# A seven-unit Strassen step for two chunks of the second sequence matrix, with its operand sums made by DMAs

## The chip, the cores and the metric

The kernel runs on one NeuronCore of a Trainium2 chip. The metric is the device time of one execution in microseconds, taken as the median of several runs. The engines are named as in the profile: PE (TensorE, matmuls), PEld (its weight loads), DVE (VectorE), ACT (ScalarE), POOL (GpSimd) and SP (SyncE, which here only issues DMAs). Each engine works off its own instructions in the order in which the program lists them, and waits on semaphores for the others.

## The reference

The function mixes two branches for S = 2048 tokens of width D = 640:

```python
x = A_x
g = sigmoid((x * gate_w).sum(-1, keepdims=True))
a = FNet(x)          # Real(DFT_seq(DFT_hid(x)))
b = PEER(x)          # product-key expert retrieval
return g * a + (1 - g) * b
```

FNet is `y = Cr (x Dr^T) - Ci (x Di^T)` with the sequence matrices Cr, Ci (2048 x 2048) and the hidden matrices Dr, Di (640 x 640). PEER makes 32 queries per token from `w_q` (640 x 32 x 256), scores each half against 16 keys, takes the best two of each half and the best two of their sums, and adds up the 2 x 32 chosen experts: `softmax(score) * gelu(x . u[e]) * v[e]`, with 256 experts of width 640.

## The kernel before

All products are done in fp32r in three parts. An operand is split by `split` (L121) into a high part (ACT rounds a copy, L123) and a low part (POOL or DVE subtracts, L124), and `mm3` (L126) multiplies high by high, high by low and low by high: three matmuls of 512 columns, L128 to L130, called a product here.

**The sequence products.** The kernel multiplies the sequence matrices with x first: for each matrix w (0 real, 1 imaginary) and each chunk c of 512 output columns, 16 pieces s. Each is one product for each of the five d tiles of x, into five PSUM banks (`seq_piece`, L201). That makes 128 pieces in `pieces` (L152). x stands split in SBUF (`X`). A piece is loaded by SP into one of five buffers `wf` (`load_piece`, L155, five pieces ahead) and split by ACT and POOL three pieces ahead (`split_piece`, L163) into a ring `WS` of four places. When a chunk ends, ACT copies the five banks to the staging tile `ST` (L218). DVE multiplies them by the gate row `grow` (`gate_piece`, L187), and ACT issues the stores to the DRAM tensor `pd[w, c]` one piece later (`store_piece`, L196).

**What lies between the pieces.** The program is one list written out by hand: `at(n, f)` puts f behind piece n. Up to piece 30 the queries' weights are folded with the keys. From N0 = 31 the score stage runs, 40 pieces long, five for each pair p of 128-token tiles. Behind each of the last four of the five stands one half of a score (`score_half`, five products, evacuated by ACT at L429), and behind the last `u_pair`, the product with the experts' `u`, and the split of the next tiles of x transposed (`split_xT`, ACT and POOL). DVE picks the best two (`topk`, L443 to L454). From N1 = 71 the hidden matrices are loaded and split into `DD` (`split_dd`, POOL). When the rows of the choices are in place (`rows`, DMA transposes issued by SP), the generator `experts` (L564) starts. DVE builds one-hot tiles (`build`, L572, three operations of 1024 columns, L579 to L581), PE multiplies them with 32-column matmuls (`use`, L599, line L607, one or two builds in a group), and ACT takes the sums out of the bank (L588).

**The pump.** What is not placed by `at` comes from `Pump`. Each product calls `run_bg(0.68)`, which adds 0.68 times `share` (0.95, or 1.25 while the experts run) to a credit. While the credit is positive the next step of the generators is put into the program, and its cost (3.3 for a build) is taken off. Other work of DVE takes its own cost off with `bg.credit -= ...`.

**The hidden products** come last, from L939 on. For each half b of the columns there is a Strassen step of seven units (`UNITS`, L671), with operand sums made by DVE (`add_a`, L747) and splits five steps ahead into a ring of six. The last pieces prepare it: `make_sums` and `split_sums` from 14 pieces before the end.

Of the kernel before, what the change touches and what calls it, by code (L numbers as in the profile page):

```python
# [16 lines left out]
P = 128  # L17
# [8 lines left out]
NP = NT // 2  # L26
TC = 512
NC = S // TC
NPC = 2 * NC * NT
KD = D // P  # L30
HALF = D // 2
NG = HH // 8
# [4 lines left out]
KX = KD + 1  # L37
NSTEP = 7 * KX
AHEAD = 5


class Pump:
# [49 lines left out]
def gated_mix_kernel(ctx: ExitStack, tc: tile.TileContext, xT, xn, dreT, dimT, wsre, wsim, wq, kT, uT, vv, gw, out):  # L92
# [25 lines left out]
    def stage():  # L118
        return ST[:, rotate("st", 5)]

    def split(f, h, l, eng):  # L121

        nc.scalar.activation(h, f, AF.Copy)  # L123
        eng.tensor_sub(l, f, h.bitcast(F32))  # L124
# [6 lines left out]

    pd = {(w, c): dram.tile([KD, P, TC], F32, name=f"pd{w}{c}", tag=f"pd{w}{c}") for w in range(2) for c in range(NC)}
    actd = dram.tile([2, P, S], F32, name="actd")
    gd = dram.tile([2, 2, 2, 2, E, E, P], F32, name="gd")
    gdr = dram.tile([S], F32, name="gdr")
    bg = Pump()
# [12 lines left out]

    pieces = [(w, c, s) for w in range(2) for c in range(NC) for s in range(NT)]  # L152
    pf, psp, X, xr = {}, {}, {}, {}

    def load_piece(n):  # L155
        if n < NPC:
            w, c, s = pieces[n]
            pf[n] = big.tile([P, TC], F32, name="wf", tag="wf", bufs=5)
            nc.sync.dma_start(pf[n], (wsre, wsim)[w][c, s])

    WS = big.tile([P, 4, 2, TC], F32R, name="WS", tag="WS")

    def split_piece(n, eng=nc.gpsimd):  # L163
        if n < NPC:
            psp[n] = WS[:, n % 4, 0], WS[:, n % 4, 1]
            split(pf.pop(n), *psp[n], eng)


    then = {}
# [31 lines left out]
    def seq_piece(n):  # L201
        w, c, s = pieces[n]
        if s == 0:
            banks[:] = [bank(d) for d in range(KD)]
# [8 lines left out]
        for d in range(KD):  # L213
            ds = slice(d * P, (d + 1) * P)
            mm3(banks[d], X[s][:, 0, ds], X[s][:, 1, ds], h, l, s == 0, s == NT - 1)
            if s == NT - 1:
                staged[n // NT, d] = f = stage()
                nc.scalar.activation(f, banks[d], AF.Copy)  # L218
            run_bg(0.68)

    for q in range(2 * NC):
        n = NT * (q + 1)
# [15 lines left out]
    def split_x(s):  # L238

        if s < NT:  # L240
            X[s] = big.tile([P, 2, D], F32R, name="X", tag=f"X{s}")
            f = xr[s // 2][:, s % 2]
            if s:
                split(f, X[s][:, 0], X[s][:, 1], nc.vector)
                return
            psp[0] = h, l = WS[:, 0, 0], WS[:, 0, 1]
            c = slice(0, 2 * P)
            split(f[:, c], X[0][:, 0, c], X[0][:, 1, c], nc.vector)
            split(pf.pop(0), h, l, nc.vector)
            c = slice(2 * P, D)  # L250
            split(f[:, c], X[0][:, 0, c], X[0][:, 1, c], nc.vector)

# [7 lines left out]
    pf[0] = big.tile([P, TC], F32, name="wf", tag="wf", bufs=5)  # L260
    nc.scalar.dma_start(pf[0], wsre[0, 0])
# [275 lines left out]
    def u_pair(p):  # L537
# [9 lines left out]
        for n in range(2):  # L547
            nc.scalar.dma_start(actd[n][:, 2 * p * P:2 * (p + 1) * P], act[:, n])

    for p in range(NP):  # L550
# [13 lines left out]
    def experts():  # L564
# [33 lines left out]

        def use(group):  # L599
            shape = (P, 16, E * 2)  # L600
            t = bank(7, shape) if last_part else ps_s(shape)
            for a, (g, c, s) in enumerate(group):
                pt, qt = (HOT[s // 2][:, s % 2, n].rearrange("p (m c j) -> p m c j", m=16, j=2) for n in range(2))
                for m in range(16):
                    for j in range(2):
                        r = slice(64 * (m % 2) + 32 * j, 64 * (m % 2) + 32 * j + 32)
                        nc.tensor.matmul(t[r, 8 * a + m // 2, :], pt[:, m, :, j], qt[:, m, :, j], start=True,  # L607
                                         stop=True)
# [121 lines left out]
    def take(key):  # L730
        if raw_tags:
            t, n = raw_tags.pop(0)
            if t == "wf":
                raw_free.append(big.tile([P, TC], F32, name="ra", tag=t, bufs=5))
# [101 lines left out]
    def step(m):  # L836
        b, (u, k) = m // NSTEP, divmod(m % NSTEP, KX)
        what = UNITS[u]
        if k == 0:
            if what in ("a11", "s1"):  # L840
                roles["W"] = bank(0)
            if what in ("a12", "a22"):
                roles["Z"] = [bank(1), bank(2)]
            if what == "s1":
                roles["Y"] = [bank(3), bank(4)]
            if what == "a11":
                roles["X"] = [bank(5), bank(6)]
# [142 lines left out]
```

## Time and profile before

| | us |
|---|---|
| median of 3 runs | 773.79 |
| lowest, highest | 772.95, 775.86 |
| the profiled execution | 773.85 |
| its span, first to last instruction | 772.1 |
| PE busy | 766.7 |
| DVE busy | 516.2 |
| POOL busy | 346.5 |
| ACT busy | 287.3 |

The time is that of one launch; the span is what lies between the first and the last instruction of the profile, 1.75 us less. A row of the groups gives line, engine and operation, the tiles written and read, count, then busy time and mean ns of one, then the engine's idle time just before and what ended it. A row of the timeline gives start, duration, engine, line, operation and tiles; `x4` means that four stand together, and the bracket tells how long the engine had idled and for whom. `SPq` and `ACTq` are DMAs issued by SP and ACT. A row of the stages gives start and end, length, busy time (and instructions) of PE, PEld, DVE, ACT and POOL, granted clock, DMA share and GB/s.

### The profile page before, as it was taken

How to read it: one execution, taken by the hardware profiler on the slowest of the kernel's cores; microseconds unless marked ns; L12 is line 12 of the kernel's file. 1: busy time of each engine (PE TensorE's matmuls, PEld its weight loads, DVE VectorE, ACT ScalarE, POOL GpSimd, SP SyncE). 2: the span in 40 equal slices, each digit the busy share in tenths (PEclk: the TensorE clock that was granted, in tenths of full speed). 3: DMA queues.
4: the chain of work that ended last, by engine and by line, in shares of the span. 5: the costliest groups of instructions: out<-in, count | busy, mean ns of one | idle time of the engine just before them, and what ended most of it. 6: DMA issues, size and time to landing. Idle time of an engine off the chain costs nothing.

```text
span 772.1 us, 11964 instructions
## 1 busy us (share of the span) xinstructions
PE 766.7 (99%) x4616; PEld 620.3 (80%) x4616; DVE 516.2 (67%) x611; ACT 287.3 (37%) x470; POOL 346.5 (45%) x235
## 2 busy tenths in 40 slices
PE   9999999999999999999999999999999999999997
PEld 6777677888888888888888888777788888788886
DVE  7642122276888698579988592677677789747761
ACT  5334324322214432353343462332243453543341
POOL 4522224315143242325242875343446765577253
PEclk9999999999999999999999999999999999999999
DMA  9976985603030440223325454453565586686411
GB/s 343 375 259 191 315 317 191 213 0 117 14 102 25 149 147 15 84 67 130 120 54 169 138 157 122 97 153 89 143 187 169 184 296 218 204 252 220 128 54 70
DMA packets 86953, 121.21 MB, mean 157 GB/s; under 512 B 33136, under 2 KB 40432, under 8 KB 86896
## 3 DMA queue, kind: packets, MB, share of 16 engines
q1 hardware_dynamic: 57360, 100.64, 39.7%
q10 hardware_dynamic: 29536, 19.81, 8.1%
q8 instruction: 36, 0.59, 0.3%
q14 instruction: 21, 0.17, 0.1%
HBM read 98.91 MB, written 19.93 MB: 154 GB/s over the span
## 4 chain that ended last, share of the span: by engine, by line
PE 98%; ACT 1%; POOL 0%; issue 0%; DVE 0%; ACTq 0%; DVEq 0%
PE b L128 31%; PE b L129 31%; PE b L130 31%; PE b L326 2%; PE b L607 1%; PE b L338 1%; PE b L211 1%; PE b L278 0%; POOL WS L124 0%; ACT L396 0%; ACT WS L123 0%; ACT ST L806 0%; ACT wp L332 0%; ACT WP L123 0%; ACT ST L218 0%
## 5 line engine op out<-in xcount | busy, mean ns | idle before, releaser
L124 POOL TENSOR_TENSOR WS<-wf,WS 128x512 fp32r<-128x512 f32 x126 | 189.6, 1509 | 279.3 <-ACT WS L123 250.3
L128 PE MATMUL b<-WS,X 128*128 128x512 f32 x635 | 251.2, 396 | 0.2 <-ACT ST L218 0.2
L129 PE MATMUL b<-WS,X 128*128 128x512 f32 x635 | 247.6, 390 | 0.0
L130 PE MATMUL b<-WS,X 128*128 128x512 f32 x635 | 247.5, 390 | 0.0
L128 PEld LDWEIGHTS b<-WS,X 128*128 128x128 f32 x635 | 119.2, 188 | 33.4 <-issue 7.3
L130 PEld LDWEIGHTS b<-WS,X 128*128 128x128 f32 x635 | 119.2, 188 | 25.4
L129 PEld LDWEIGHTS b<-WS,X 128*128 128x128 f32 x635 | 119.3, 188 | 23.5
L123 ACT ACTIVATE WS<-wf 128x512 fp32r<-128x512 f32 x128 | 80.6, 630 | 113.7 <-PE b L130 57.2
L443 DVE TENSOR_REDUCE mm<-sc 128x64 f32<-128x1024 f32 x32 | 39.0, 1219 | 46.3 <-ACT sc L429 45.7
L124 POOL TENSOR_TENSOR xl<-xf,xh 128x640 fp32r<-128x640 f32 x16 | 33.6, 2123 | 70.4 <-ACT xh L123 64.0
L124 POOL TENSOR_TENSOR WS<-ra,WS 128x512 fp32r<-128x512 f32 x40 | 59.7, 1512 | 12.0 <-ACT WS L123 12.0
L130 PE MATMUL b<-WU,xl 128*128 128x512 f32 x160 | 62.2, 389 | 0.0
L128 PE MATMUL b<-WU,xh 128*128 128x512 f32 x160 | 62.2, 389 | 0.0
L129 PE MATMUL b<-WU,xh 128*128 128x512 f32 x160 | 62.2, 389 | 0.0
L429 ACT ACTIVATE sc<-b 128x512 f32<-128x512 f32 x32 | 21.1, 661 | 100.4 <-PE b L130 93.5
L579 DVE TENSOR_TENSOR hot<-rows,wtab 128x1024 f16<-128x1024 f16 x32 | 30.0, 938 | 36.9 <-PE b L607 36.9
L123 ACT ACTIVATE WS<-ra 128x512 fp32r<-128x512 f32 x56 | 34.8, 630 | 51.8 <-PE b L130 29.8
L124 POOL TENSOR_TENSOR WP<-ra,WP 128x512 fp32r<-128x512 f32 x20 | 32.5, 1636 | 45.2 <-ACT WP L123 45.1
L749 DVE TENSOR_TENSOR ra<-ra 128x512 f32<-128x512 f32 x48 | 45.6, 1002 | 4.2 <-POOL WP L124 4.2
L192 DVE SCALAR_TENSOR_TENSOR ST<-ST,grow 128x512 f32<-128x512 f32 x40 | 37.1, 992 | 15.9 <-DMA grow<-gdr 15.9
L341 DVE TENSOR_TENSOR WU<-b,WU 128x512 fp32r<-128x512 f32 (+1 forms) x16 | 7.8, 490 | 57.2 <-ACT WU L340 57.2
L445 DVE TENSOR_TENSOR eq<-sc,mm 128x1024 f16<-128x1024 f32 x32 | 44.4, 1388 | 1.1
(132 smaller groups left out, 1182.4 us busy)
## 6 DMA issues: line engine op xcount, KB each, us to landing
wq<-in_wq SPq DMA_DIRECT2D x32, 640.0 KB, 6.7
ra<-pd SPq DMA_DIRECT2D x70, 256.0 KB, 3.7
wf<-in_wsim SPq DMA_DIRECT2D x64, 256.0 KB, 2.9
wf<-in_wsre SPq DMA_DIRECT2D x63, 256.0 KB, 5.4
pd<-ST ACTq DMA_DIRECT2D x40, 256.0 KB, 3.1
xf<-in_xT SPq DMA_DIRECT2D x16, 320.0 KB, 3.2
xr<-in_xn SPq DMA_DIRECT2D x15, 320.0 KB, 6.4
out_y<-ST ACTq DMA_DIRECT2D x7, 512.0 KB, 3.8
```

The source lines that it names most:

```text
L123: nc.scalar.activation(h, f, AF.Copy)
L124: eng.tensor_sub(l, f, h.bitcast(F32))
L128: nc.tensor.matmul(o, wh, ah, start=first, stop=False, skip_group_check=more)
L129: nc.tensor.matmul(o, wh, al, start=False, stop=False, skip_group_check=more)
L130: nc.tensor.matmul(o, wl, ah, start=False, stop=last, skip_group_check=more)
L192: nc.vector.scalar_tensor_tensor(f, f, -1.0 if w else 1.0, g, op0=OP.mult, op1=OP.mult)
L326: nc.tensor.matmul(ps[32 * j:32 * j + 32, :HALF], kp[:, 8 * G // H, r, :], w[:, j], start=(r == 0), stop=(r == 1))
L429: nc.scalar.activation(scs[i].rearrange("p h e -> p (h e)")[:, c], ps, AF.Copy)
L443: nc.vector.tensor_reduce(m, sc, op=OP.max, axis=AX.X)
L445: nc.vector.tensor_tensor(eq, sc, m[:, :, None].to_broadcast([P, HH, E]), op=OP.is_equal)
L579: nc.vector.tensor_tensor(pt, row(0), wt, op=OP.is_equal)
L749: nc.vector.tensor_add(take((b, o, k)) if f is not None else raw[b, o, k], raw[b, o, k] if f is None else f, raw[b, what, k])
```

## The change

The chunks are taken in another order: the four of the first matrix, then chunk 2 of the second, then chunks 0 and 1 of the second together, then chunk 3. The pair of chunks is a 2 x 2 block problem: output chunk (0, 1) times the half of the s tiles (0 to 7, 8 to 15). d tiles 0 and 1 against 2 and 3 of x make the other operand's halves. It is done with seven products of half blocks instead of eight, the units `QUNITS`, each with eight steps k of two d tiles. d tile 4 is done as before, a third product in the steps of four units. So 32 pieces become 56 steps (`quad_step`), and the list has 152 entries instead of 128 (Q0 = 80 to Q1 = 136 are the steps).

The units need sums of blocks of the sequence matrix (four, `sd`) and of x (four, `td`). They are made in the score stage, one k for each pair of tiles (`sums_part`). Two `wf` buffers are loaded by SP, ACT negates one, POOL issues DMAs that add a block from DRAM onto a buffer (`accum_op`), and SP stores each finished sum to DRAM. The sums of x are four subtractions on DVE, stored by one DMA. In the steps the sums are loaded like pieces, those of x in a ring of five, and split by ACT with POOL or DVE.

Beside that: the `wf` buffers become a queue of tags, to which two are added when the experts start, and the steps and later pieces are loaded seven ahead. The experts' sums always use bank 7. The last part of `DD` is split by DVE. The last chunk uses banks 3, 4, 5, 6, 0, and the hidden products swap two pairs of banks.

```diff
+HN = NT // 2
+Q0 = 5 * NT
+Q1 = Q0 + 7 * HN
+NPC = Q1 + NT
+QUNITS = ("a11", "a12", "s1", "s2", "s4", "s3", "a22")
...
+    order = ((0, 0), (0, 1), (0, 2), (0, 3), (1, 2))
+    pieces = [(w, c, s) for w, c in order for s in range(NT)] + [None] * (Q1 - Q0) + [(1, 3, s) for s in range(NT)]
...
     def load_piece(n):
-        if n < NPC:
-            w, c, s = pieces[n]
-            pf[n] = big.tile([P, TC], F32, name="wf", tag="wf", bufs=5)
-            nc.sync.dma_start(pf[n], (wsre, wsim)[w][c, s])
+        nonlocal loaded
+        while loaded <= min(n, NPC - 1):
+            pf[loaded] = wf_tile("wf")
+            nc.sync.dma_start(pf[loaded][0], source(loaded))
+            load_t(loaded)
+            loaded += 1
...
     def split_piece(n, eng=nc.gpsimd):
         if n < NPC:
             psp[n] = WS[:, n % 4, 0], WS[:, n % 4, 1]
-            split(pf.pop(n), *psp[n], eng)
+            f, tag = pf.pop(n)
+            if Q0 <= n < Q1 and unit(n)[0] in ("s1", "s2", "s4") and n % 3 == 0:
+                eng = nc.vector
+                bg.credit -= 0.9
+            split(f, *psp[n], eng)
+            wf_tags.append(tag)
+            split_t(n)
...
-        load_piece(n + 5)
+        load_piece(n + (7 if p3 else 5))
...
+    def split_t(n):
+        if t_index(n) is None:
+            return
+        m = qs["m"] % 4
+        qs["m"] += 1
+        f = tq[n]
+        tq[n] = [qs["hl"][m // 2][:, m % 2, a] for a in range(2)]
+        split(f, *tq[n], nc.vector)
+        bg.credit -= 0.5
...
+    def q_out(name, o, r, dp):
+        f, g = qres[name], grow[NC + r]
+        for a in range(2):
+            nc.vector.tensor_tensor(f[:, a], f[:, a], qrole[o][a], op=OP.add)
+            nc.vector.scalar_tensor_tensor(f[:, a], f[:, a], -1.0, g, op0=OP.mult, op1=OP.mult)
+        bg.credit -= 2.8
+        nc.scalar.dma_start(pd[1, r][2 * dp:2 * dp + 2].rearrange("d p t -> p d t"), f)
...
+    def quad_step(n):
+        what, k = unit(n)
...
+        load_piece(n + 7)
+        split_piece(n + 3)
+        h, l = psp.pop(n)
+        o = {"a11": "X", "a12": "Z", "s1": "Y", "s2": "X", "s4": "Y", "s3": "X", "a22": "Z"}[what]
...
+        for d in ds:
+            if d < 2:
+                c = slice(d * P, (d + 1) * P)
+                mm3(qrole[o][d], t[0][:, c], t[1][:, c], h, l, k == 0 and not more, end, more)
+            else:
+                c = slice(4 * P, KD * P)
+                mm3(qrole["W"], wx[:, 0, c], wx[:, 1, c], h, l, k == 0 and low, end and what != "s3", what == "a12")
+            run_bg(0.68)
+        if end:
+            q_post(what)
...
+    def sums_add(f, r, s):
+        nc.gpsimd.dma_start(f, wsim[r, s], accum_op=OP.add)
...
+    def sums_part(k, i):
+        if i == 0:
+            sums_load(k)
+        elif i == 1:
+            sums_neg(k)
+            sums_add(sb[k], 1, k + HN)
+            sums_x(k)
+        elif i == 2:
+            sums_add(sa[k], 1, k)
+            sums_store(sb[k], 0, k)
+            nc.sync.dma_start(td[k].rearrange("p j c -> p (j c)"), sx.pop(k).rearrange("p n c -> p (n c)"))
+        elif i == 3:
+            sums_store(sa[k], 2, k)
+        elif i == 4:
+            sums_add(sa[k], 1, k + HN)
+        elif i == 5:
+            sums_store(sa[k], 1, k)
+        elif i == 6:
+            sums_neg(k)
+        elif i == 7:
+            sums_add(sa[k], 0, k + HN)
+        elif i == 8:
+            sums_store(sa[k], 3, k)
...
     for p in range(NP):
         n = N0 + 5 * p
-        for a in range(4):
-            at(n + 1 + a, score_half, 2 * p + a // 2, a % 2)
+        for a in range(5):
+            at(n + a, sums_part, p, 2 * a)
+            if a:
+                at(n + a, score_half, 2 * p + (a - 1) // 2, (a - 1) % 2)
+            at(n + a, sums_part, p, 2 * a + 1)
...
-            t = bank(7, shape) if last_part else ps_s(shape)
+            t = bank(7, shape)
...
-        split(draw[m][:, a], DD[:, w, 0, k], DD[:, w, 1, k], nc.gpsimd)
+        split(draw[m][:, a], DD[:, w, 0, k], DD[:, w, 1, k], nc.vector if m == KD - 1 else nc.gpsimd)
```

`q_post` stands at a unit's end. It copies banks to `ST` with ACT (units a11, s1, s2, s3) or calls `q_out` (a12, s4, s3, a22); after a12 and a22, d tile 4 goes out as well.

More of the change, by code (lines that the diff above doesn't have):

```diff
@@ L148, in gated_mix_kernel, with wf_tile, unit, source @@
     gt = const.tile([P, NT], F32)
-    pieces = [(w, c, s) for w in range(2) for c in range(NC) for s in range(NT)]
+    order = ((0, 0), (0, 1), (0, 2), (0, 3), (1, 2))
+    pieces = [(w, c, s) for w, c in order for s in range(NT)] + [None] * (Q1 - Q0) + [(1, 3, s) for s in range(NT)]
     pf, psp, X, xr = {}, {}, {}, {}
-    def load_piece(n):
-        if n < NPC:
-            w, c, s = pieces[n]
-            pf[n] = big.tile([P, TC], F32, name="wf", tag="wf", bufs=5)
-            nc.sync.dma_start(pf[n], (wsre, wsim)[w][c, s])
+    wf_tags = deque((big, f"wf{n}") for n in range(5))
+    def wf_tile(name):
+        pool, tag = wf_tags.popleft()
+        return pool.tile([P, TC], F32, name=name, tag=tag), (pool, tag)
+    def unit(n):
+        u, k = divmod(n - Q0, HN)
+        return QUNITS[u], k
+    def source(n):
+        if not Q0 <= n < Q1:
+            w, c, s = pieces[n]
+            return (wsre, wsim)[w][c, s]
+        what, k = unit(n)
+        if what[0] == "s":
+            return sd[int(what[1]) - 1, k]
+        return wsim[int(what[1]) - 1, k + HN * (int(what[2]) - 1)]
+    loaded = 0
+    def load_piece(n):
+        nonlocal loaded
[4 more added lines that the diff above has]
+            loaded += 1
     WS = big.tile([P, 4, 2, TC], F32R, name="WS", tag="WS")
@@ L203, in seq_piece @@
         if s == 0:
[L204 to L205 removed]
+            banks[:] = [bank(d) for d in ((3, 4, 5, 6, 0) if n >= Q1 else range(KD))]
+        load_piece(n + (7 if p3 else 5))
         split_piece(n + 3)
@@ L212, in seq_piece @@
             return
-        for d in range(KD):
+        for d in ((4, 0, 1, 2, 3) if n == NPC - 1 else range(KD)):
             ds = slice(d * P, (d + 1) * P)
@@ L216, in seq_piece, with t_index, load_t @@
             if s == NT - 1:
-                staged[n // NT, d] = f = stage()
+                staged[w * NC + c, d] = f = stage()
                 nc.scalar.activation(f, banks[d], AF.Copy)
             run_bg(0.68)
-    for q in range(2 * NC):
-        n = NT * (q + 1)
+    tq, qs = {}, {}
+    def t_index(n):
+        what = unit(n)[0] if Q0 <= n < Q1 else None
+        return {"s1": 0, "s3": 1, "a22": 2, "s2": 3}.get(what)
+    def load_t(n):
+        j = t_index(n)
+        if j is None:
+            return
+        if not qs:
+            qs["raw"] = big.tile([P, 5, 2 * P], F32, name="tr", tag="xl")
+            qs["hl"] = [big.tile([P, 2, 2, 2 * P], F32R, name="tq", tag=t) for t in ("xf", "xh")]
+            qs["n"] = qs["m"] = 0
+        tq[n] = qs["raw"][:, qs["n"] % 5]
+        qs["n"] += 1
+        nc.sync.dma_start(tq[n], td[unit(n)[1], :, j])
@@ new lines, in q_post @@
+    def q_post(what):
+        if what == "a11":
+            nc.scalar.activation(qres["w"], qrole["W"], AF.Copy)
+            q_copy("c", "X")
+        elif what == "a12":
+            f = p3.tile([P, TC], F32, name="wrow")
+            nc.vector.scalar_tensor_tensor(f, qrole["W"], -1.0, grow[NC], op0=OP.mult, op1=OP.mult)
+            nc.scalar.dma_start(pd[1, 0][4], f)
+            q_out("c", "Z", 0, 0)
+        elif what == "s1":
+            q_copy("c22", "Y")
+        elif what == "s2":
+            q_copy("c", "X")
+        elif what == "s4":
+            q_out("c", "Y", 0, 1)
+            grow.pop(NC)
+        elif what == "s3":
+            q_copy("c", "X")
+            q_out("c22", "X", 1, 1)
+        else:
+            f, g = qres["w"], grow[NC + 1]
+            nc.vector.tensor_tensor(f, f, qrole["W"], op=OP.add)
+            nc.vector.scalar_tensor_tensor(f, f, -1.0, g, op0=OP.mult, op1=OP.mult)
+            nc.scalar.dma_start(pd[1, 1][4], f)
+            q_out("c", "Z", 1, 0)
+            grow.pop(NC + 1)
@@ new lines, in quad_step @@
+    def quad_step(n):
+        what, k = unit(n)
+        if k == 0:
+            if what in ("a11", "s3"):
+                qrole["W"] = bank(0)
+            if what in ("a12", "a22"):
+                qrole["Z"] = [bank(1), bank(2)]
+            if what == "s1":
+                qrole["Y"] = [bank(3), bank(4)]
+            if what == "a11":
+                qrole["X"] = [bank(5), bank(6)]
+        load_piece(n + 7)
+        split_piece(n + 3)
+        h, l = psp.pop(n)
+        o = {"a11": "X", "a12": "Z", "s1": "Y", "s2": "X", "s4": "Y", "s3": "X", "a22": "Z"}[what]
+        low = what in ("a11", "s3")
+        wx = X[k if low else HN + k]
+        if what in ("a11", "a12"):
+            t = [wx[:, a, :2 * P] for a in range(2)]
+        elif what == "s4":
+            t = [wx[:, a, 2 * P:4 * P] for a in range(2)]
+        else:
+            t = tq.pop(n)
+        more = what in ("s2", "s4", "s3")
+        end = k == HN - 1
+        ds = [0, 1]
+        if what not in ("s1", "s2", "s4"):
+            ds = [2] + ds if end else ds + [2]
+        for d in ds:
+            if d < 2:
+                c = slice(d * P, (d + 1) * P)
+                mm3(qrole[o][d], t[0][:, c], t[1][:, c], h, l, k == 0 and not more, end, more)
+            else:
+                c = slice(4 * P, KD * P)
[3 more added lines that the diff above has]
+            q_post(what)
```

54 lines of the change are left out of this document (45 added, 9 removed).

## The prediction

> **What bounds the kernel now.** I read the page's busy time and chain of waits first, then the timeline of TensorE, then the groups of the engines that feed it.
>
> ```profile
> span 772.1 us, 11964 instructions
> ...
> PE 766.7 (99%) x4616; PEld 620.3 (80%) x4616; DVE 516.2 (67%) x611; ACT 287.3 (37%) x470; POOL 346.5 (45%) x235
> ...
> PE 98%; ACT 1%; POOL 0%; issue 0%; DVE 0%; ACTq 0%; DVEq 0%
> ```
>
> TensorE is never without work: 99% busy, and 98% of the chain that ended last. So the time is the number of matmuls times their spacing, and a matmul that goes is worth its spacing, unless TensorE then waits for what it multiplies. The spacing isn't the mean of the group (390 ns, matmuls overlap); it is the distance of starts in the timeline:
>
> ```profile
> 599.81 0.39 PE L128 MATMUL b<-WS,X 128*128 128x512 f32 x1
> ...
> 600.49 0.39 PE L128 MATMUL b<-WS,X 128*128 128x512 f32 x1
> ```
>
> Between these rows stand one L129 and one L130, so three matmuls take 0.68 us: 0.227 each, 0.68 a product (one mm3), 3.40 a piece of five.
>
> **What goes.** Chunks 0 and 1 of the second matrix are 2 x 16 pieces x 15 = 480 matmuls. In their place stand 56 steps (seven units, k = 0 to 7) of two products, and a third for d tile 4 in a11, a12, s3 and a22: 56 x 6 + 32 x 3 = 432. That is 48 fewer, 48 x 0.227 = **10.9 us**. The profiled execution took 773.85 us (its span 772.1 and 1.75 around it), 0.06 above the median, so without a stall: 773.85 - 10.9 = 763.0.
>
> **What comes, and what hides it.** A step without d tile 4 lasts 1.36 us on TensorE, with it 2.04, where a piece lasted 3.40. Each still needs its split, prepared only three steps ahead (the ring WS has four places), so the lead shrinks from 10.2 us to 4.1 or 6.1:
>
> ```profile
> L124 POOL TENSOR_TENSOR WS<-wf,WS 128x512 fp32r<-128x512 f32 x126 | 189.6, 1509 | 279.3 <-ACT WS L123 250.3
> ...
> L123 ACT ACTIVATE WS<-wf 128x512 fp32r<-128x512 f32 x128 | 80.6, 630 | 113.7 <-PE b L130 57.2
> ```
>
> ACT 0.63 and POOL 1.51 are 2.1 us of latency: it fits, with 2 us over, if nothing stands ahead of them. Three things do.
>
> *The first steps.* When piece 79 has ended, DVE gates chunk (1,2) and ACT issues its five stores; ACT's next splits queue behind them.
>
> ```profile
> 447.58 0.63 ACT L123 ACTIVATE WS<-wf 128x512 fp32r<-128x512 f32 x1 [1.08 <-POOL DD L124]
> ...
> 450.19 4.72 ACTq L199 DMA_DIRECT2D pd<-ST  x4
> 454.95 0.74 ACT L123 ACTIVATE DD<-draw 128x640 fp32r<-128x640 f32 x1 [4.90 <-DVE hot L579]
> 455.60 0.61 ACT L123 ACTIVATE WS<-wf 128x512 fp32r<-128x512 f32 x1
> ```
> ```profile
> 457.62 1.75 POOL L124 TENSOR_TENSOR WS<-wf,WS 128x512 fp32r<-128x512 f32 x1
> 459.32 2.02 POOL L124 TENSOR_TENSOR DD<-draw,DD 128x640 fp32r<-128x640 f32 x1
> ```
>
> By their order these are the splits for piece 84 (447.58, when piece 80 ends) and piece 85, which POOL finishes at 459.4. TensorE wants it four pieces after 447.6, at 461.2: 1.8 us to spare. With steps of 2.04 it would want it at 447.58 - 1.36 + 4 x 2.04 = 454.4, 5.0 us too early if nothing on ACT moves. If the issues (1.2 us each here, beside SP's transposes) went at once, the loss is 0. I take 2.5, half, since one row is all there is, and keep 0 and 5.0.
>
> *POOL against DVE.* Rows of DVE from the same stretch:
>
> ```profile
> 458.14 1.78 DVE L581 TENSOR_TENSOR hot<-hot,rows 128x1024 f16<-128x1024 f16 x1
> 459.84 2.06 DVE L579 TENSOR_TENSOR hot<-rows,wtab 128x1024 f16<-128x1024 f16 x1
> ```
> ```profile
> 453.75 0.68 DVE L579 TENSOR_TENSOR hot<-rows,wtab 128x1024 f16<-128x1024 f16 x1
> 454.35 0.68 DVE L580 TENSOR_TENSOR hot<-rows,wtab 128x1024 f16<-128x1024 f16 x1
> ```
> ```profile
> 472.08 1.29 POOL L124 TENSOR_TENSOR WS<-wf,WS 128x512 fp32r<-128x512 f32 x1 [1.61 <-ACT WS L123]
> ```
>
> Alone a DVE operation takes 0.68 (0.60 from start to start) and POOL's split 1.29. Together each ends when the other's has, and a pair takes 1.7 us (457.62 to 459.32): the two don't overlap, and a DVE operation costs the pair 0.45 to 0.60. The Trainium skill, "SBUF — State Buffer", section "Who interferes with whom", has the rule: a DVE instruction with two SBUF inputs and a GpSimd instruction that reads SBUF exclude each other for the whole instruction; the rows agree.
>
> So I add both engines up over the 56 steps. TensorE: 32 x 2.04 + 24 x 1.36 = 97.9 us, and the experts' small matmuls, which a group of two builds puts in between:
>
> ```profile
> 484.65 0.39 PE L130 MATMUL b<-WS,X 128*128 128x512 f32 x1
> 484.97 0.68 PE L607 MATMUL b<-hot 128*32 128x32 f16 x64
> 485.58 0.50 PE L128 MATMUL b<-WS,X 128*128 128x512 f32 x1
> 485.92 0.39 PE L129 MATMUL b<-WS,X 128*128 128x512 f32 x1
> ```
>
> Two matmul starts lie 1.27 us from 484.65 to 485.92 instead of 0.45: 0.82 a group. How many builds? Each product grants 0.68 x 1.25 = 0.85 credit; from step 84, about where the experts can start, 132 products give 112. Away go 32 x 0.5 (splits of the x sums), 8 x 0.9 (pieces split on DVE) and 4 x 2.8 (outputs): 78 remain, at 3.4 a build 23 builds, 12 groups. TensorE's total: 97.9 + 9.6 = 107.5 us.
>
> The pair: POOL 48 x 1.29 + 2 x 1.6 for DD = 65; DVE 69 operations for builds, 8 piece splits, 14 gatings and 2 for DD, 93 x 0.45 to 0.60 = 42 to 56; 32 splits of 256 columns at half that, 7 to 10. Sum 114 to 131 us, **6 to 23 over TensorE**. About 3.5 us of it once is slack (the lead of 4.1 less a share of the latency); the rest stalls TensorE, as builds and splits stand ahead of its own matmuls. Against the upper end speaks a stage as full as this that shows no stall:
>
> ```profile
> 632.00:720.00 88.00, 87.92 (x386) 71.81 (x385) 64.26 (x70) 36.67 (x62) 61.25 (x39) 1.00 0.66 215
> ```
> ```profile
> L749 DVE TENSOR_TENSOR ra<-ra 128x512 f32<-128x512 f32 x33 | 31.7, 1013 | 4.2 <-POOL WP L124 4.2
> L788 DVE TENSOR_TENSOR ra<-ra 128x512 f32<-128x512 f32 x6 | 8.5, 1416 | 0.1
> L789 DVE TENSOR_TENSOR ra<-ra 128x512 f32<-128x512 f32 x6 | 8.0, 1341 | 0.2
> L124 DVE TENSOR_TENSOR WS<-ra,WS 128x512 fp32r<-128x512 f32 x8 | 7.3, 917 | 1.2 <-ACT WS L123 1.2
> ...
> L124 DVE TENSOR_TENSOR WP<-ra,WP 128x512 fp32r<-128x512 f32 x4 | 3.3, 837 | 5.2 <-ACT WP L123 5.2
> ```
>
> 39 x 1.29 and 57 x 0.45 to 0.60 are 76 to 84 of 88 us, and TensorE was busy for 87.92. I take the lower end, since where both queues are full the rows say 0.45: 6 - 3.5, **2.5 to 3**; I put 3.0, and keep 0 and 19.
>
> *Ends of units.* q_out makes DVE do two additions from PSUM and two gatings, and ACT waits with its store before it goes on to the next splits:
>
> ```profile
> L192 DVE SCALAR_TENSOR_TENSOR ST<-ST,grow 128x512 f32<-128x512 f32 x40 | 37.1, 992 | 15.9 <-DMA grow<-gdr 15.9
> ```
> ```profile
> L810 DVE TENSOR_TENSOR ST<-ST,b 128x512 f32<-128x512 f32 x14 | 9.2, 683 | 18.4 <-ACT ST L806 12.8 <-PE b L130 5.6
> ```
>
> 2 x 0.68 + 2 x 0.99 = 3.3 us, of which the first half can run before the unit's last product ends: ACT is free about 2.6 after it, then 0.5 to issue, 0.63 and a split on DVE or POOL of 0.7 to 1.5: 4.4 to 5.2. After a12 the lead is 4.1 us, so 0.3 to 1.1 late, or 2 more behind a build; after s4, s3 and a22 the lead is 6.1 and more. I take 0.8, and keep 0 and 4.
>
> *The operand sums* lie in the score stage, one pair of x tiles at a time.
>
> ```profile
> L546 ACT ACTIVATE ST<-b x8: 598/598/599, 173.9 to 413.5; 128x512 f32<-128x512 f32 x8
> ```
> ```profile
> wf<-in_wsim SPq DMA_DIRECT2D x64, 256.0 KB, 2.9
> ...
> pd<-ST ACTq DMA_DIRECT2D x40, 256.0 KB, 3.1
> ```
> ```profile
> L443 DVE TENSOR_REDUCE mm<-sc 128x64 f32<-128x1024 f32 x31 | 37.8, 1219 | 35.4 <-ACT sc L429 34.8
> ```
>
> The period is (413.5 - 173.9) / 7 = 34.2 us. One buffer goes through load (2.9), two negations (0.63), three stores (3.1) and three accumulating DMAs of A us; some ten hand-overs I estimate at 2 us: 15.5 + 3A. No row shows A; the nearest is 2.9 to 3.1, and even twice that, 6.2, fits 34.2. SP waits for each accumulation before it issues the store, with the next piece's load behind it; POOL waits for the store before, with splits behind it; ACT for the negation. A piece and a half score take 6.8 us there, so three pieces of lead are 20 us and hide it: 0. DVE's 32 subtractions (about 11 us) fit the 34.8 in which it waited for scores. The Trainium skill, "DMA: Bandwidth & Descriptors", section "Anatomy of one DMA — SWDGE (gpsimd) path", gives 2.0 us and bytes over 436 GB/s for a plain DMA of POOL, an estimate of 2.6 here: the sum would be the same.
>
> *Loads.* In s1 and s2 a step brings 256 and 128 KB in 1.36 us, 289 GB/s.
>
> ```profile
> 0.00:40.00 40.00, 38.83 (x187) 28.35 (x191) 26.27 (x36) 17.55 (x29) 19.82 (x20) 1.00 0.93 355
> ```
>
> 355 GB/s have been moved, so with seven buffers I take 0, and keep 3.
>
> **The sum.** 773.85 - 10.9 + 2.5 + 3.0 + 0.8 = **769.3 us**, faster by 0.6%. A measurement of this kernel can tell about 0.5%, 3.9 us, from no change.
>
> **The rivals.**
> - *The stalls return the gain* (no change): the first steps cost their 5.0 and the pair's sum lies in the middle, 122.5, 15 over and 11.5 after slack: 763.0 + 5 + 11.5 - some overlap of the two (5) = 774. For it: POOL alone fills 63% of every step. Against: the full stage above.
> - *POOL and DVE become the bound* (slower): at 0.60 an operation the pair needs 131 us, and 23 - 3.5 + 2.5 + 0.8 make 763.0 + 22.8 = 786. It decides from the sum of 122 us on, 0.52 an operation. The exclusion that the Trainium skill states ("SBUF — State Buffer", "Who interferes with whom") leads here when no operation of DVE is cheaper beside POOL than alone; the trace has both, 0.45 and 0.60.
> - *The accumulation is slow* (slower): from A = 6.2 us the chain of a pair outlasts its period. At 8 us, 8 x (39.5 - 34.2) - 20 = 22 us: 785. Nothing in the profile speaks for it; nothing excludes it.
> - That the matmuls don't go is excluded: the count is in the code.
>
> **How the numbers follow.** Forecast, stalls up to 7 us (763 to 769.9): 0.46. Gain returned (770 to 777.7): 0.29. Pair as the bound 0.17, slow accumulation 0.08: 0.25 slower. The range leaves out the far tail of the slower cases: 763 to 785.
>
> **What would show it.** Right: 4568 or so matmuls; TensorE with gaps only near the start of a11 and in s1 and s2, where POOL's and DVE's means rise above 1.5 and 0.8; the score stage without gaps. Wrong: gaps in each 34.2 us period with SP waiting for an accumulation; gaps before L607 all through the 56 steps (the builds are late); or TensorE gaps on "DMA wf". What would upset all of it is a loss of clock after a gap (now 1.00).

## The result and the profile after

The changed kernel takes 848.18 us (median of 4 runs, 845.45 to 851.07), the kernel before 773.40 beside it: a ratio of 1.096, with a 95% interval of 1.0915 to 1.1005. The forecast was 769.3 with a range to 785.0. The change is **slower by almost a tenth**.

The page of the profiled execution after (851.07 us): busy time and the chain of waits.

```profile
span 849.3 us, 12425 instructions
...
PE 783.4 (92%) x4568; PEld 623.7 (73%) x4568; DVE 598.8 (71%) x694; ACT 316.4 (37%) x544; POOL 384.1 (45%) x281
...
PE 24%; DVE 13%; DMA 6%; issue 5%; POOL 4%; ACT 1%; SPq 1%; ACTq 0%; DVEq 0%; POOLq 0%
```

The matmuls went as counted, 4568. But TensorE's share of the chain fell from 98% to 24%. Its busy time rose although it does less: a matmul at a lower clock is busy for longer, and the mean granted clock is 0.968 where it was 0.999.

Where the time lies is best seen by stages, cut at events that both kernels have: the first and the last gelu (the score stage), the last evacuation of a chunk's banks (the sequence stage with the seven units), and the end (the hidden products). First the kernel before, then after; columns as in the stages shown earlier.

```profile
173.90:413.50 239.60, 239.60 (x1156) 202.52 (x1156) 198.41 (x214) 84.94 (x115) 86.12 (x49) 1.00 0.27 86
413.50:620.40 206.90, 206.90 (x1880) 168.41 (x1879) 147.74 (x192) 80.82 (x140) 112.55 (x79) 1.00 0.51 148
620.40:772.10 151.70, 147.71 (x648) 120.97 (x646) 99.87 (x111) 60.12 (x102) 87.62 (x57) 1.00 0.54 181
```
```profile
174.60:449.20 274.60, 250.50 (x1167) 208.62 (x1166) 225.19 (x239) 90.20 (x129) 102.65 (x77) 0.96 0.61 166
449.20:682.30 233.10, 206.85 (x1629) 163.34 (x1629) 193.66 (x229) 101.04 (x194) 132.17 (x93) 0.94 0.57 173
682.30:849.30 167.00, 153.09 (x840) 123.19 (x838) 109.57 (x128) 62.05 (x108) 87.83 (x57) 0.98 0.53 173
```

Before, TensorE is busy for the whole of the first two stages at a clock of 1.00. After, all three stages are longer: the score stage by 35.0 us, the sequence stage by 26.2, the hidden products by 15.3, and 0.7 lies ahead of them. That is the 77.2 us between the spans. Since the sequence stage should have become 10.9 shorter, 88.1 us have to be explained: **35.0 + 37.1 + 15.3 + 0.7**.

What TensorE waited for in the score stage of the kernel after (total, times, longest), and what SP waited for there:

```profile
PE b L132 <- ACT ST L254: 16.4, 2, 9.1
PE b L132 <- ACT sc L579: 7.7, 6, 3.6
```
```profile
SPq L717 <- DMA sa<-in_wsim: 64.2, 17, 6.9
SPq L509 <- POOL xl L128: 46.3, 6, 12.8
SPq L717 <- DMA sb<-in_wsim: 42.4, 7, 7.8
```

TensorE never waits for a split piece there (`WS`), but for banks that ACT has not yet emptied: L254 is the evacuation of a chunk, L579 that of a score. And SP, which issues nearly all loads, stands still for 153 us of this stage: for accumulations that it is to store (L717), and for POOL's split of x transposed (L509, `load_xT` of the next pair but one).

One of these gaps in full, in the timelines of SP, ACT and TensorE (a bracket: how long the engine had idled, and for whom):

```profile
245.31 0.33 SPq L717 DMA_DIRECT2D sd<-sa  x1
252.26 0.81 SPq L509 DMA_DIRECT2D xf<-in_xT  x2
...
254.12 0.38 SPq L705 DMA_DIRECT2D sa<-in_wsim  x1
```
```profile
261.12 0.63 ACT L711 ACTIVATE sa<-sa 128x512 f32<-128x512 f32 x1 [12.41 <-issue]
...
262.18 2.52 ACT L254 ACTIVATE ST<-b 128x512 f32<-128x512 f32 x5
```
```profile
255.12 0.39 PE L134 MATMUL b<-WU,xl 128*128 128x512 f32 x1
262.81 0.79 PE L132 MATMUL b<-WS,X 128*128 128x512 f32 x1 [7.30 <-ACT ST L254]
263.40 0.63 PE L133 MATMUL b<-WS,X 128*128 128x512 f32 x1
263.82 0.63 PE L134 MATMUL b<-WS,X 128*128 128x512 f32 x1
```

SP stands for 6.6 us behind the store at L717, until POOL has freed a buffer for x transposed. The load of A (`sa`) stands behind it in SP's queue and is issued only at 254.12, among seven other loads (252.26 to 257.4), and it lands 6.9 us after its issue (2.7 in the median of e2, further on). ACT stands for 12.41 us at the negation of A, L711; the profile names no releaser, but the wait ends as A has landed. Behind the negation stands the evacuation of five banks. So TensorE, whose banks they are, is idle for 7.30 us. Then, from 263.40 on, its matmuls start 0.42 to 0.43 us apart, not 0.227: it has lost half its clock as well.

In the 56 steps the picture is another. DVE, POOL and TensorE around 567 us, at the start of s3:

```profile
565.57 1.77 DVE L786 TENSOR_TENSOR hot<-rows,wtab 128x1024 f16<-128x1024 f16 x1
567.26 1.74 DVE L787 TENSOR_TENSOR hot<-rows,wtab 128x1024 f16<-128x1024 f16 x1
568.92 0.68 DVE L788 TENSOR_TENSOR hot<-hot,rows 128x1024 f16<-128x1024 f16 x1
569.52 1.08 DVE L128 TENSOR_TENSOR tq<-tr,tq 128x256 fp32r<-128x256 f32 x3
```
```profile
560.24 8.22 POOL L128 TENSOR_TENSOR WS<-wf,WS 128x512 fp32r<-128x512 f32 x5 [0.85 <-ACT WS L127]
```
```profile
566.85 0.40 PE L133 MATMUL b<-WS,tq 128*128 128x512 f32 x1
569.99 0.62 PE L134 MATMUL b<-WS,tq 128*128 128x512 f32 x1 [2.75 <-DVE tq L128]
```

Five splits of POOL run end to end (8.22 us), and each operation of a build beside them takes 1.74 to 1.77 us instead of 0.68, the duration once POOL is done. The splits of the x sums, `tq`, stand behind two builds in DVE's queue, and TensorE waits for them. And at the end of a12, where `q_out` empties the banks (L295, L296) and ACT waits to issue the store (L298):

```profile
527.56 0.63 ACT L127 ACTIVATE WS<-wf 128x512 fp32r<-128x512 f32 x1 [8.14 <-DVE ST L296]
```
```profile
524.12 0.39 PE L134 MATMUL b<-WS,tq 128*128 128x512 f32 x1
528.54 0.50 PE L132 MATMUL b<-WS,tq 128*128 128x512 f32 x1 [4.03 <-ACT tq L127]
```

### The profile page after: what moved, and what is told of

Same layout as the page of the kernel before. It is cut to its first block, busy times and chain, and to the rows that moved or that the text cites. A ratio compares the mean times of both kernels' runs of the same rounds, so it can differ in the third digit from the quotient of the medians.

```text
span 849.3 us, 12425 instructions
## 1 busy us (share of the span) xinstructions
PE 783.4 (92%) x4568; PEld 623.7 (73%) x4568; DVE 598.8 (71%) x694; ACT 316.4 (37%) x544; POOL 384.1 (45%) x281
## 4 chain that ended last, share of the span: by engine, by line
PE 24%; DVE 13%; DMA 6%; issue 5%; POOL 4%; ACT 1%; SPq 1%; ACTq 0%; DVEq 0%; POOLq 0%
PE b L134 8%; PE b L132 8%; PE b L133 8%; POOL WS L128 3%; DVE hot L788 2%; DMA ra<-pd 2%; DVE hot L786 2%; DVE ra L956 1%; DMA out_y<-ST 1%; POOL WP L128 1%; DMA ra<-gd 1%; DVE tq L128 1%; DVE hot L787 1%; POOL DD L128 1%; DMA gd<-cd 1%
## 5 line engine op out<-in xcount | busy, mean ns | idle before, releaser
L128 POOL TENSOR_TENSOR WS<-wf,WS 128x512 fp32r<-128x512 f32 x142 | 210.9, 1493 | 197.7 <-ACT WS L127 168.0
L132 PE MATMUL b<-WS,X 128*128 128x512 f32 x555 | 223.7, 403 | 20.7 <-ACT ST L254 16.6
L133 PE MATMUL b<-WS,X 128*128 128x512 f32 x555 | 220.4, 397 | 3.6 <-POOL WS L128 3.6
L134 PE MATMUL b<-WS,X 128*128 128x512 f32 x555 | 219.4, 395 | 0.0
L132 PEld LDWEIGHTS b<-WS,X 128*128 128x128 f32 x555 | 106.5, 192 | 53.0 <-ACT ST L254 17.9
L127 ACT ACTIVATE WS<-wf 128x512 fp32r<-128x512 f32 x152 | 94.8, 629 | 100.6 <-issue 25.3
L133 PEld LDWEIGHTS b<-WS,X 128*128 128x128 f32 x555 | 106.7, 192 | 26.0 <-POOL WS L128 4.8
L134 PEld LDWEIGHTS b<-WS,X 128*128 128x128 f32 x555 | 106.4, 192 | 22.9
L128 POOL TENSOR_TENSOR WS<-ra,WS 128x512 fp32r<-128x512 f32 x40 | 59.6, 1509 | 29.4 <-ACT WS L127 29.3
L714 POOL DMA_DIRECT2D sa<-in_wsim x24 | 23.5, 980 | 79.5 <-DMA sd<-sa 27.4
L127 ACT ACTIVATE WS<-ra 128x512 fp32r<-128x512 f32 x56 | 34.8, 630 | 61.4 <-DVE ra L956 26.6
L128 POOL TENSOR_TENSOR xl<-xf,xh 128x640 fp32r<-128x640 f32 x16 | 31.2, 1970 | 49.6 <-ACT xh L127 39.4
L659 ACT ACTIVATE rows<-rt 128x384 f16<-128x384 f16 x16 | 31.1, 1943 | 45.9 <-DMA rt<-gs 45.9
L956 DVE TENSOR_TENSOR ra<-ra 128x512 f32<-128x512 f32 x48 | 41.6, 913 | 6.8 <-DMA ra<-pd 6.8
L711 ACT ACTIVATE sa<-sa 128x512 f32<-128x512 f32 x16 | 10.1, 632 | 85.2 <-issue 59.6
```

What stands on the lines that cost most here:

```text
L132: nc.tensor.matmul(o, wh, ah, start=first, stop=False, skip_group_check=more)
L133: nc.tensor.matmul(o, wh, al, start=False, stop=False, skip_group_check=more)
L134: nc.tensor.matmul(o, wl, ah, start=False, stop=last, skip_group_check=more)
L659: nc.scalar.activation(ROWS[i // 8][:, :, :, i % 8], t, AF.Copy)
L714: nc.gpsimd.dma_start(f, wsim[r, s], accum_op=OP.add)
L956: nc.vector.tensor_add(take((b, o, k)) if f is not None else raw[b, o, k], raw[b, o, k] if f is None else f, raw[b, what, k])
```

## The experiments

Each is the changed kernel with one edit; e5 and e6 add theirs to that of e2, e9 to e11 carry several, and e12 is the kernel before. All are single executions, set against the profiled execution after (851.07 us) by the same three stages; the kernel before took 772.2 to 774.8 us on the same chips. How far a stage moves by itself is seen where the edit lies in another: the score stage took 272.8 to 274.6 us in four such runs (after, e4, e7, e8), the sequence stage 229.5 to 233.7 in five (after, e2, e3, e5, e6), the hidden products 165.5 to 167.2 in six (these five and e7).

| | score | sequence | hidden | time, us |
|---|---|---|---|---|
| before | 239.6 | 206.9 | 151.7 | 773.85 |
| after | 274.6 | 233.1 | 167.0 | 851.07 |
| e1, no operand sums | 239.5 | 229.9 | 167.3 | 812.94 |
| e2, loads earlier | 256.3 | 231.0 | 167.0 | 830.22 |
| e3, negation by POOL | 274.3 | 229.5 | 165.5 | 845.04 |
| e5, e2 and stores by POOL | 247.2 | 232.9 | 165.5 | 821.73 |
| e6, e2 and plain copies | 248.4 | 233.7 | 167.2 | 824.23 |
| e4, builds with one input | 272.8 | 214.7 | 166.2 | 829.21 |
| e7, stores later | 273.0 | 228.3 | 167.2 | 844.24 |
| e8, no experts | 273.5 | 193.6 | 151.9 | 794.75 |
| e9 = e5 and e7 | 247.1 | 228.7 | 168.4 | 820.34 |
| e10 = e9, larger share | 246.8 | 238.1 | 152.8 | 813.96 |
| e11 = e9, no experts | 245.9 | 194.6 | 152.2 | 768.50 |
| e12, before without experts | 239.5 | 193.8 | 151.7 | 760.98 |

### The score stage

My theory was the order of SP's queue, as in the gap above. The rivals: ACT's negation by itself, or accumulating DMAs that are too long.

**e1, no operand sums**

```diff
-            at(n + a, sums_part, p, 2 * a)
...
-            at(n + a, sums_part, p, 2 * a + 1)
```

> Left out: the operand sums in the score stage; the steps load blocks of the same size from the inputs instead. In the changed kernel the score stage (first to last L696) takes 274.6 us against 239.6 before. If the sums cost that, it takes 240 to 242 here, and the time falls by 33 to 36 us to 812 to 816. If the new order of the pieces or the load queue cost it, it stays over 260. The 56 steps and the rest should lose what they lost.

```profile
173.70:413.20 239.50, 239.50 (x1156) 202.47 (x1155) 198.38 (x214) 84.88 (x115) 86.27 (x49) 1.00 0.27 86
```

The score stage of e1 is that of the kernel before, 239.5 us, TensorE busy throughout at full clock. So all 35.0 us come from the sums. The sequence stage became only 3.2 us shorter, which is within its spread: its loss is not a late consequence of the score stage.

**e2, the loads of the next pair's sums behind this pair's last store**

```diff
         if i == 0:
-            sums_load(k)
+            if k == 0:
+                sums_load(0)
...
+            if k + 1 < NP:
+                sums_load(k + 1)
```

> The loads of a pair's sums are issued behind the last store of the pair before, ahead of the load of x transposed that waits for POOL. Theory 1 (the order of SP's queue: the loads come late and ACT stands at its negation): ACT's wait of 59.6 us ahead of L711 goes, and of the 35 us lost in the score stage under 10 are left; time 820 to 826. Theory 2 (the chain of three accumulating DMAs is too long for a pair): the stage stays within 5 us of 274.6.

The stage took 256.3 us: 18.3 of the 35.0 came back by nothing but another place in SP's queue. ACT's 59.6 us ahead of L711 are gone, but 16.7 us are left, where theory 1 expected under 10. The largest gap of e2 is still one at ACT's evacuation, now of 4.1 us where 9.1 was.

**e3, the negation on POOL**

```diff
-        nc.scalar.activation(sa[k], sa[k], AF.Copy, scale=-1.0)
+        nc.gpsimd.tensor_scalar(sa[k], sa[k], -1.0, None, op0=OP.mult)
```

> The negations are done by POOL instead of ACT; the loads come as late as before. Theory 1a (what costs is that ACT, with the banks to empty behind it, stands at the negation): of the 35 us lost in the score stage under 12 are left, time 822 to 828. Theory 1b (everything is late because the loads and stores on SP are late): the stage stays above 265, with POOL's splits as what TensorE waits for.

Nothing came back (274.3). What ACT waited for in the score stage at the copies of the choices' rows, after and then in e3:

```profile
ACT rows L659 <- DMA rt<-gs: 44.9, 11, 7.1
```
```profile
ACT rows L659 <- DMA rt<-gs: 70.5, 12, 12.8
```

ACT now stands at these copies, whose transposes SP issues too, for 25.6 us more. It is not the negation that stops ACT, but whatever of its queue waits next for a late SP. TensorE still waits for ACT's evacuations (21.6 us) and not, as theory 1b had it, for POOL's splits.

**e5, e2 with the stores of the sums issued by POOL**

```diff
-        nc.sync.dma_start(sd[j, k], f)
+        nc.gpsimd.dma_start(sd[j, k], f)
```

> As e2, and the stores of A's sums are issued by POOL, so that SP never waits for an accumulation. e2's score stage takes 256.3 us, 16.7 over before, with ACT waiting for DMA transposes (rt) that stand behind such waits on SP. Theory 1b (SP's order): under 7 of the 16.7 are left, stage 240 to 246, time 814 to 820. Theory 2 (the accumulations' length): within 4 us of 256.3.

With this, SP waits for no accumulation any more. 247.2 us: 27.4 of the 35.0 are gone, and 7.6 are left, a little more than the 7 expected. SP still stands for 166 us of the stage, against 178 for all reasons in the kernel after, but its longest waits are now for the buffers of pieces that POOL has yet to split (61.4 us). So it isn't the total of SP's waiting that costs, but what stands behind it.

**e6, e2 with plain copies in place of the accumulations**

```diff
-        nc.gpsimd.dma_start(f, wsim[r, s], accum_op=OP.add)
+        nc.gpsimd.dma_start(f, wsim[r, s])
```

> As e2, with plain copies by POOL in place of the accumulations (the sums are not made). Theory 2: the stage falls from 256.3 to under 247, and issue to landing of these DMAs is well under the 4.3 us of e2. Theory 1b: within 4 us of 256.3, since SP waits for plain copies as well.

Issue to landing of POOL's DMAs onto A, first in the kernel after, then in e6:

```profile
sa<-in_wsim POOLq DMA_DIRECT2D x24, 256.0 KB, 4.4
```
```profile
sa<-in_wsim POOLq DMA_DIRECT2D x24, 256.0 KB, 3.0
```

The sum that an accumulating DMA makes on its way costs 1.2 to 1.4 us: 4.2 in e2 and 4.4 in the kernel after, against 3.0 (onto B, 5.8 in e2 against 4.5). I had expected this not to matter once the loads are early, and that was wrong: the stage took 248.4 us, 7.9 less than e2, though not under the 247 of theory 2. But e5 reaches the same with the accumulations at full length, so by these runs their length costs time because SP waits for them with the loads behind.

### The sequence stage

**e4, builds with one SBUF input.** The three operations of a build become reductions of about the same duration.

```diff
-            nc.vector.tensor_tensor(pt, row(0), wt, op=OP.is_equal)
-            nc.vector.tensor_tensor(qt, row(1), wt, op=OP.is_equal)
-            nc.vector.tensor_tensor(pt, pt, row(2), op=OP.mult)
+            p0, q0 = (HOT[s // 2][:, s % 2, n] for n in range(2))
+            for o, i in ((p0, q0), (q0, p0), (p0, q0)):
+                nc.vector.tensor_reduce(o[:, :64], i[:, 512:].rearrange("p (a b) -> p a b", b=8), op=OP.max, axis=AX.X)
```

> The experts' three operations of a build are replaced by three reductions of 512 elements of about the same length, with one input (the one-hot tiles are not built). Theory 3 (DVE and POOL exclude each other where DVE has two inputs): what lies from the last L696 to the last bank emptied of the sequence products, 233.1 us against 206.9 before, falls by 15 or more, and POOL's mean over the 56 steps comes under 1.4 us. Theory 4 (DVE's order and length of work: splits stand behind builds and outputs) : it falls by under 8.

The groups of the builds in the sequence stage, after and then e4:

```profile
L787 DVE TENSOR_TENSOR hot<-rows,wtab 128x1024 f16<-128x1024 f16 x28 | 33.3, 1188 | 0.0
L786 DVE TENSOR_TENSOR hot<-rows,wtab 128x1024 f16<-128x1024 f16 x28 | 28.4, 1016 | 4.5 <-PE b L814 4.4
```
```profile
L788 DVE TENSOR_REDUCE hot<-hot 128x64 f16<-128x512 f16 x84 | 51.8, 674 | 19.8 <-POOL hot L1139 15.8 <-PE b L814 4.1
```

Both have 28 builds there (the reductions are 3 x 28). The reductions take 0.67 us each beside POOL, the two-input operations of L786 and L787 1.02 and 1.19 in the mean, and 0.68 alone. The stage fell from 233.1 to 214.7 us: **18.4 us** (15 to 19 against the five runs of this stage) are the price of builds and POOL's splits not overlapping. POOL's mean for the split of a piece fell from 1.50 to 1.39 us, as theory 3 expected, and one of TensorE's waits is gone altogether, which in the kernel after was:

```profile
PE b L134 <- DVE tq L128: 9.2, 4, 2.7
```

The Trainium skill, "SBUF — State Buffer", section "Who interferes with whom", says that a DVE instruction with at most one SBUF input, outside the two-port modes, doesn't contend with GpSimd, and that `tensor_reduce` never does on this chip; the 0.67 us agrees.

**e7, the stores of chunk (1,2) at Q0 + 4 instead of Q0 + 1, and `q_out`'s store four steps later**

```diff
-        at(n + (8 if q == 0 else 1), store_piece, q)
+        at(n + (8 if q == 0 else 4 if q == 6 else 1), store_piece, q)
...
-        nc.scalar.dma_start(pd[1, r][2 * dp:2 * dp + 2].rearrange("d p t -> p d t"), f)
+        at(now + 4, lambda: nc.scalar.dma_start(pd[1, r][2 * dp:2 * dp + 2].rearrange("d p t -> p d t"), f))
```

> ACT issues the stores of chunk (1,2) three steps later and those of q_out three steps later, when DVE has long been done; all else as changed. Theory 4a (ACT stands at stores, the splits behind it): the gaps of 7 us at the start of a11 and of 4.2 after a12 go; from the last L696 to the last bank emptied 233.1 us fall by 8 to 14, time 834 to 840. Theory 3 alone (POOL against DVE): under 4.

The stage took 228.3 us, 4.8 less than in the profiled execution after, but only 1.2 less than the shortest of the five runs in which this stage is as it was, and 3.7 less than their mean. So a gain is not shown clear of their spread. Theory 4a (8 to 14) is not met; theory 3 alone (under 4) would fit the mean. The gap of 4.2 us after a12 is gone, but gaps of 1.5, 2.7 and 1.2 stand near its place, and the 7 us at the start of a11 are 6. The five stores still hold ACT for 5.60 us, against 7.23 in the kernel after, with splits behind them: they come later, but they have not left the queue.

**e8, no experts**

```diff
-            bg.add(experts(), late=True)
+            summed.update((0, 1))
```

> Left out: the experts' builds, matmuls and sums. The hidden products, from the last bank emptied to the end of the span, take 167.0 us against 151.7 before. Theory 5 (what is left of the experts falls into them): 151 to 155 here. Rival (the new banks, loads or splits cost it): over 160. From the last L696 to the last bank emptied, before takes 206.9 with 13 us of expert matmuls; less these and 10.9 it would be 183. Theory 3: under 197; what is over 183 is ACT at its stores and POOL's own splits.

The sequence stage fell by 39.5 us to 193.6, and the hidden products by 15.1 to 151.9. By itself this doesn't tell what the experts lose, since their own matmuls take time too; that needs e12.

**e12, the kernel before without experts**

> The kernel before, without the experts in the same way. Theory: before the change they were hidden entirely, TensorE ran through the sequence stage at full rate: 206.9 us of that stage and 151.7 of the hidden one stay within 2, time within 2 us of 773 less the 16 or fewer us of TensorE that the experts' own matmuls take, if these take any on the path. Rival: they cost the kernel before as well, and the fair measure of the change without experts is this time, 760 or less.

```profile
413.70:607.50 193.80, 193.80 (x856) 160.45 (x855) 72.85 (x98) 71.96 (x124) 104.51 (x79) 1.00 0.46 145
```

TensorE is at full rate through the whole stage, but the stage did not stay at 206.9: the experts cost the kernel before 13.1 us there (206.9 - 193.8), which is the time of their own matmuls, 16 groups at the 0.82 of the prediction. So after the change they cost 39.5 - 13.1 = 26.4 us more in this stage. And without experts the changed kernel needs 193.6 us where the kernel before needs 193.8: 48 matmuls are gone, and **10.7 of the 10.9 us are lost without the experts**.

**e11, e9 without experts, shows where**

> The three edits and no experts: their builds, sums and matmuls are left out, and the hidden products load act in place of gd. Theory of three separate losses: score stage 247 us, sequence stage 193.6 less 5, hidden stage 152: some 765 us, 8 below the kernel before, which would be what is left of the 48 matmuls saved. Rival: the seven units' ends lose the gain by themselves whatever stands beside them: 772 or more.

Three stretches of e11, from the end of chunk (1,2) to s1, and the wait that cost TensorE most in the sequence stage:

```profile
440.00:460.00 20.00, 18.77 (x83) 15.26 (x82) 14.10 (x11) 10.86 (x19) 20.00 (x15) 1.00 0.56 183
460.00:480.00 20.00, 16.21 (x55) 11.96 (x55) 7.58 (x5) 11.39 (x16) 13.16 (x9) 0.83 0.62 184
480.00:500.00 20.00, 18.08 (x78) 14.37 (x78) 11.13 (x15) 9.62 (x18) 9.90 (x7) 1.00 0.70 220
500.00:520.00 20.00, 20.00 (x90) 16.56 (x89) 12.21 (x16) 14.22 (x28) 13.05 (x10) 1.00 0.89 288
```
```profile
PE b L133 <- POOL WS L128: 3.4, 3, 1.3
```

A full stretch of 20 us holds 90 matmuls; these three hold 83, 55 and 78. 54 are missing, at 20/90 us each 12.0. TensorE waits for split pieces: POOL is busy for all of the first 20 us, since DVE's five gatings stand beside its splits and those of `DD` between them, while a step of a11 lasts 2.04 us and not 3.40. Then, from 465.00 to 469.89, ACT issues the five stores with three splits behind them, and TensorE waits for these next. I made no run without the splits of `DD`, so how the 12 us divide is not shown. From 500 us on nothing is missing in the units. Against the fair comparison, e12 (760.98), e11 at 768.50 is still slower. Its score stage is 6.4 us longer, its sequence stage 0.8. That refutes the reading I had written ahead of it, that 8 us below the kernel before would be what is left of the gain.

### Together, and the experts' share

**e9, e5 and e7 together**

> Loads of the sums ahead of part 8, their stores issued by POOL, and the stores of chunk (1,2) and of the unit ends four steps later, together. If the two losses are separate (SP's order in the score stage, ACT standing at stores in the sequence stage) they add: the run of the early loads with POOL's stores took 821.7 us, that of the later stores 6.8 us less than the changed kernel, so 815 within 3 us. Rival: both free the same waiting of DVE and the experts, so that the second gives nothing behind the first: 820 or more.

820.34 us, what the rival had: the score stage keeps its 27.5, the sequence stage is 4.2 shorter than in e5, but the hidden products take 168.4, 2.9 more than in e5. The first difference is no larger than the spread of its stage (4.2), the second a little larger than that of its own (1.7). The builds' first operation in e9, with the first and last start at its end:

```profile
L792 DVE TENSOR_TENSOR hot<-rows,wtab x32: 673/681/1802, 467.7 to 729.0; 128x1024 f16<-128x1024 f16 x32
```

The builds reach 79 us into the hidden products, which begin at 649.9.

**e10, e9 with a share of 1.75**

```diff
-        share = 0.95 if p3 is None or ending else 1.25
+        share = 0.95 if p3 is None or ending else 1.75
```

> The same with a share of 1.75 in place of 1.25 for the background work in the steps of chunks 0 to 3. Theory: in these steps DVE has no room left for the experts, so that a larger share only moves the loss from the hidden products into the sequence stage: hidden stage nearer to 152 us than to 166, sequence stage longer by as much or more, time within 5 us of the run with 1.25 or above it. Rival: there is room and the credit merely holds the experts back: hidden stage down by 10 us or more, sequence stage longer by less than half of it, time at least 5 us below.

```profile
L792 DVE TENSOR_TENSOR hot<-rows,wtab x32: 677/680/1782, 466.5 to 605.5; 128x1024 f16<-128x1024 f16 x32
```

The last build begins at 605.5, none reaches the hidden products, and these are back at 152.8 us: the 15 us there are the rest of the experts. The sequence stage pays 9.4 of the 15.6 back. That is neither expectation in full; the credit did hold the experts back, and the steps had no free room for them either. At 813.96 us it is the fastest version that computes everything, and still 5% above the kernel before.

## Why the prediction was wrong, point by point

**The matmuls** (-10.9): right. 4568 were counted. Their spacing at full clock is unchanged, as the 90 a stretch in e11 show.

**The operand sums** (0): wrong, and the largest error, 35.0 us. The sentence that failed is "three pieces of lead are 20 us and hide it: 0". It looked at the chain of one buffer, and that chain does fit: A is 4.4 us, below the 6.2 at which the rival of slow accumulation began. But the lead protects only split pieces, and TensorE never waited for these in the score stage. It waited for banks, and the evacuation of a bank has no lead: whatever ACT waits for ahead of it, TensorE waits for as well. I had named the queues (SP ahead of loads, ACT at the negation) and not followed ACT's queue to the evacuations at L254 and L579, nor SP's to the load of x transposed, which itself waits for POOL. e2 and e5 show that it is order: 27.4 of the 35.0 go when the loads of the sums stand ahead of x transposed and SP waits for no accumulation. The last 7.6 us of e5 stay open in part. Its one long wait of TensorE, 4.0 us, is again for the evacuation at L254, and I made no run that takes it away.

**POOL against DVE** (3.0): the right mechanism, its size wrong. e4 measures 18.4 (15 to 19), close to the 23 - 3.5 = 19.5 of the rival "POOL and DVE become the bound". I had taken the lower end, 0.45 us an operation, because a stage as full showed no stall. That stage has leads of five steps; here a build that takes 1.74 to 1.77 us an operation delays the `tq` splits behind it, and TensorE waits with only three steps of lead.

**The first steps** (2.5) **and the ends of units** (0.8): 10.7 without experts, against an upper end of 5.0 + 4 = 9. e11 puts nearly all of it at the start of a11, where two things are seen: ACT's stores ahead of its splits, which the prediction named, and a POOL that is full (20.00 of 20.00 us), with DVE's gatings beside it, which it counted only in its sum over the 56 steps. No run separates the two; e7, which moved the stores, gained 1 to 5 us. Of the experts' further 26.4 us, e4 explains 18.4; the other 8.0 I did not separate.

**The experts' remainder** was not priced at all: 15.3 us in the hidden products, shown by e8 and e10. I had counted that 23 builds get credit in the 56 steps, and had not asked where the rest go when the pieces that hosted them are gone. In the kernel before, the last build began at 565.3 us, 55 us ahead of the hidden products:

```profile
L579 DVE TENSOR_TENSOR hot<-rows,wtab x32: 675/692/2058, 449.6 to 565.3; 128x1024 f16<-128x1024 f16 x32
```

**The clock** stood last, as what "would upset all of it", without a price, and it did upset it. I added up in the timeline what lies between the starts of TensorE's neighbouring matmuls beyond 0.227 us. Where one starts 0.05 to 0.34 us late, these are 6.2 us in the score stage, 14.0 in the sequence stage and 2.9 in the hidden products, against 0, 3.0 and 0.8 in the kernel before: 19 us more, the clock's part. Longer gaps are 26, 30 and 11 us (6 of the 11 ahead of the experts' matmuls), against none before. Together that is 86 of the 88 us, and by this estimate, which counts short waits with the clock, a gap is paid for by three tenths more than it lasts. The prediction's terms were gaps alone.

## What to carry to other kernels

When a step is moved into a stage that was full, follow each queue that it enters to the instructions that have no lead. An evacuation behind a waiting instruction can stop TensorE (7.30 us in the gap shown), however far ahead the loads are. Put a wait for a transfer on the queue that has the least behind it: loading the sums earlier and giving their stores from SP to POOL was worth 27 us. And work that was hidden beside the steps that are taken away must be given a new place in the sum, before the steps' own gain is counted.

## What the hardware showed that I had not expected

**Short gaps cost the clock.** In the kernel after a wait of 2.11 us is enough:

```profile
584.81 0.39 PE L133 MATMUL b<-WS,tq 128*128 128x512 f32 x1
587.30 0.79 PE L134 MATMUL b<-WS,tq 128*128 128x512 f32 x1 [2.11 <-DVE tq L128]
587.89 0.63 PE L132 MATMUL b<-WS,tq 128*128 128x512 f32 x1
588.32 0.63 PE L133 MATMUL b<-WS,tq 128*128 128x512 f32 x1
...
590.46 0.51 PE L132 MATMUL b<-WS,X 128*128 128x512 f32 x1
```

The starts lie 0.43 us apart from 587.89 to 590.46: seven matmuls, where the next ones come at the old spacing. Eleven such stretches of 2 to 5.5 us follow the gaps of that execution. The Trainium skill, "TensorE: Matmul & The Clock Gate", section "Part 1: The HAM clock gate (the "warmup" mystery)", states half the clock after an idle window of about 3.4 us, and as long until it is back; the factor agrees, and 2 to 5.5 us are near that length, but here gaps of 2.5 us, from start to start, did it.

**An accumulating DMA** of POOL takes 4.2 to 4.4 us from issue to landing (onto A), a plain one of the same 256 KB in the same place 3.0. And POOL itself is held for 0.98 us by each, by the plain one for 0.56:

```profile
L714 POOL DMA_DIRECT2D sa<-in_wsim x24 | 23.5, 980 | 79.5 <-DMA sd<-sa 27.4
```
```profile
L714 POOL DMA_DIRECT2D sa<-in_wsim x24 | 13.3, 555 | 53.7 <-DMA sd<-sa 25.4 <-ACT sa L711 25.2 <-PE b L134 2.6
```

The first row is of the kernel after, the second of e6.
